# Attention and MLP on one core: the first loads in a row on one queue, the bulk loads held until a first product, less warm work

## The chip, the cores and the metric

The kernel runs on one core of a Trainium2 chip. A core has a matrix engine (TensorE, PE in the profile), a vector engine (VectorE, DVE), an activation engine (ScalarE, ACT), a general engine (GpSimd, POOL) and a queue engine (SyncE, SP). Each works through its own instructions in order. PE writes to PSUM, and DVE and ACT read from there. SP, ACT and POOL issue DMAs, each on a queue of its own, and all queues use the same 16 DMA engines.

The metric is the device time of one execution in microseconds, as the median of several runs. Lower is better.

## The reference: what is computed

```python
# q, k, v: (8, 12, 448, 64) float32;  w_in: (768, 2048);  w_out: (2048, 768)
scores = (1 / sqrt(64)) * (q @ k.transpose(0, 1, 3, 2))
attn = maximum(scores, 0) ** 2 / 448
x = (attn @ v).transpose(0, 2, 1, 3).reshape(3584, 768)
h = x @ w_in
out = (0.5 * h * (1 + erf(h / sqrt(2)))) @ w_out        # (3584, 768) float32
```

There are eight batches of twelve heads. There is no softmax: the scores are clipped at zero and squared. The result of attention, with the heads side by side, goes through an MLP with an exact GELU.

## The kernel before, in words

**Tiling.** The twelve heads of a batch make three groups (g = 0, 1, 2) of four heads. Each group has seven key blocks of 64 rows for each head. q and k must lie with the head dimension on the partitions, so they are transposed: for batches 0 and 1 on PE, as products with an identity matrix `ident` (lines 676, 680, 708 and 715), with a copy from PSUM to SBUF behind each (line 566 on DVE); for the later batches by the DMA engines. A step of attention is one product of k and q into PSUM (line 819), one clipping on ACT (line 831) or on DVE (line 833), and one squaring on DVE (line 841). After seven steps, the products with v follow (line 881). The MLP's first layer stands in line 940, plain blocks of its second in line 1399, and grouped forms of both layers behind.

**The order of the work.** All work after the start is given as operations to `Scheduler`, numbered in the order in which they are added. `ORDER` (lines 91 to 171) is a hand-fixed list of these numbers, each with a letter for its engine: P is PE, A is ACT, D is DVE, G is POOL, S is SP, and Z is a filler product of so many columns on PE. `place()` (line 359) takes the words one after the other, so that each engine's instructions stand in the order of its words. The times in the operations (such as 4.95 in line 1502) are the planner's own estimates and due times; with every operation named in `ORDER`, they change no instruction.

**The bulk loads.** POOL issues the loads that turn float32 into bfloat16 on the way: k (line 605), q (line 514), v (line 623), w_in (lines 529 to 531), w_out (line 535). Its order begins G0 (k of group 1), G1 (q of group 1), G7 (the second half of the sequence of q of group 0), G4 (q of group 2), G108 (q of batch 1, group 0), then `make_ident()`, G2 (v of group 0), G3 (k of group 2). Each load uses one of eight semaphores in turn, so the ninth waits for the first.

**The first loads.** The first half of q of group 0 and the k of group 0 do not go through POOL. They come as float32 through the queues of SP and ACT into `q32` and `k32` (lines 1450 to 1453). k comes in two pieces, key blocks 0 to 3 (`first`, `K_CUT = 4`) and 4 to 6 (`rest`). ACT casts q (A10), DVE the first piece of k (D13) and ACT the rest (A16).

**The first steps.** P11 transposes that half of q (line 708), and D12 copies it to `qT`. P14 and P17 transpose the two pieces of k (line 676), and D15 and D18 copy them to `kT`. P29, P32, P35 and P38 are the products of the first half of q with the seven key blocks, two blocks each and one in P38; A30, A33 and A36 clip the first three and D39 the last. P19 (line 680) and P21 (line 715) transpose k and q of group 1, which G0 and G1 bring; D20 and D22 copy them. P27 does so for the second half of q of group 0. P62 is the first product of group 1, and A63 clips it. On PE the order is P11, P14, P17, P29, P32, P38, P19, P21, P35, P27, P62; on ACT A10, A16, A30, A33, A36, A63; on DVE D13, D12, D15, D18, D39, D20, D22.

**Warm work.** While the first loads are under way, PE runs `SPIN = 11` products of a zero matrix of 512 columns (line 1472), and then the filler Z1056, three products on a quarter of the array with 1056 columns in all (line 1626).

**The identity.** DVE clears `ident` at the start (line 1456), and POOL sets its diagonal by an `affine_select` (line 1459), which stands in its order behind the five loads.

**The weights of the second layer.** G222, G223 and G225 load w_out in three parts; G223 and G225 are two DMAs each. The first readers of all three parts are the plain blocks of output columns 0 to 383 (line 1399, third and fourth block in time). G261 and G262 load k and q of batch 3, group 1.

Of the kernel before, what the change touches and what calls it, by code (L numbers as in the profile page):

```python
# [8 lines left out]
F32 = mybir.dt.float32  # L9
# [3 lines left out]
B, H, S, D = 8, 12, 448, 64  # L13
# [28 lines left out]
NB = 512  # L42
# [45 lines left out]
SPIN = 11  # L88
# [3 lines left out]
D13 G0 Z1056 A10 G1 G7 G4 A16 G108 G1469 P11 D12 P14 D15 P17 P29 P32 D18 P38 D39 P19 P21 A30 D20 P35  # L92
D22 P27 A33 P62 D31 P77 A36 D40 D28 A63 P59 D34 P44 P25 G2 G3 A78 A60 D37 D45 G111 P121 P65 A66 P71
A72 P47 P74 A75 D79 A48 D122 D64 D67 P23 D73 P50 D24 D26 P68 G107 P41 A51 P98 A69 D76 A99 D61 D52
D70 P53 P123 G5 G115 G112 A42 A43 G8 G116 A54 G6 P95 P86 A96 A87 P80 D46 D124 A81 A82 P89 P92 P119
D55 D97 D49 D90 P125 P83 A93 A84 D120 P56 G109 G110 G113 P152 D126 D88 G135 D85 A57 A153 P101 P127
A58 A102 D91 P129 P143 D94 D100 D103 P158 A144 A159 P104 A105 A106 G132 P146 D130 D147 D128 S213
P229 P170 P182 D183 G9 A230 P155 A171 D154 A156 P227 G114 P140 A141 D160 P194 P164 D165 A195 A228
P237 P149 P173 G131 P200 G134 P239 A238 P241 D145 A150 A201 A174 D148 D157 A240 P176 A177 D151 D142
D172 P161 D184 A162 A242 D166 P179 P167 P235 P233 D175 D178 D163 D180 P197 P206 G118 A168 A236 D169  # L100
A198 D181 A234 P185 D207 P203 A186 P188 P231 A187 A232 P243 D214 G221 P247 A244 S212 A248 D202 D204
P249 A250 P245 D189 A246 P257 P272 D199 D205 P191 P269 D192 A258 A273 A270 G117 P255 A256 D190 G138
P251 P266 D196 D193 S215 P275 A276 D208 S216 D267 A252 P209 A210 P281 P284 A211 P356 P340 A282 G133
D217 D285 P290 P305 P308 D291 D292 A357 P342 G137 G260 A341 A309 P344 G259 G136 D283 D306 A343 A345
P253 P299 P293 P278 D268 D286 D279 D280 D271 A254 P350 A351 P352 A353 P358 A359 S219 D220 P346 A347
D300 D301 D277 P362 A363 P366 P364 P302 D294 S218 D274 D295 P317 D303 P287 A318 A367 P329 P296 A365
A288 D310 A330 D304 D307 D289 D297 P360 A361 P354 A355 G222 P370 G223 G225 G261 P326 S389 D390 P314
A315 P332 D333 A327 P372 P323 S388 P320 G262 A321 G264 G224 A371 D380 D298 P311 P439 S392 D324 D328
D322 D381 P430 P368 D383 A373 D384 A312 D334 D313 D316 A369 P348 A349 P338 A431 A339 P377 D382 A378
D385 A440 P411 S395 A412 G139 P445 D387 G226 A446 D325 D441 D407 G399 D386 P436 D331 D408 P433 P374  # L110
A375 A437 A434 P415 G263 G403 D393 D409 S391 P413 P457 P460 A461 S379 D319 D414 P335 P442 D458 P451
A336 A416 A452 P417 P419 D459 A443 A337 S394 D432 D396 D447 D418 D410 P454 P463 D420 P427 A428 P421
P423 P475 G265 D435 D553 D438 A455 A464 D429 P466 D444 G398 P448 D424 A476 D467 D422 G400 D456 G405
P478 P484 P521 G404 G397 G402 A485 D479 D462 D468 D477 A449 P525 D465 D453 A522 S532 A450 P469 P481
D533 A526 P487 A488 A470 P511 A482 S531 P517 P493 D471 P490 S538 P472 D494 D495 D483 S535 A491 A512
G540 D473 G401 A518 D474 P606 P594 P529 A607 A595 P519 A530 P597 P591 P603 A520 P527 D551 D552 D489
A604 D480 D605 A528 G545 P501 A502 P513 A514 D592 D608 D598 S534 P505 A506 G542 P507 P600 D492 D593
P609 D486 P496 A610 D536 A508 A497 D601 G406 A498 P627 P630 D631 P523 A628 D602 A524 S537 S539 P615
P618 P633 P503 P509 D632 A619 G548 D611 A634 A504 D635 P515 D629 A510 D596 P499 P621 D599 A616 S376
A500 A622 P624 G541 D625 P612 A516 A613 S696 D620 P657 D614 D617 D626 P645 A658 S702 G550 P555 A646  # L120
A556 G544 D554 S426 S695 P557 P559 D697 S425 D623 P757 S699 G710 P639 P636 A758 D640 G547 P648 D558
A560 P760 D637 A761 P561 A638 P563 D641 D562 G708 D700 G705 D659 P654 A649 D650 G706 P772 P651 A773
D564 D571 A655 P565 A652 D566 D573 D572 P567 D568 P766 P754 P642 A643 A767 D656 G546 G549 S698 G709
P575 D653 D644 P577 P769 D774 D768 D647 S701 A576 A755 P778 A779 D770 D762 P660 P763 G712 P790 A764
A661 A791 P579 D578 S569 P581 D756 P787 P793 D771 D574 A580 A662 P796 A794 A797 D582 D765 D780 D792
A788 P583 S703 D759 D584 D789 P585 P808 G543 G707 S827 P802 A803 P775 P784 S829 G842 D809 P781 D586
P587 P669 S826 D795 D828 A782 D783 G837 A776 A777 D798 A785 D714 A670 P805 S830 P814 A815 D786 D806
S833 P799 P811 D810 D588 P817 S831 S570 D800 D801 D804 P667 A818 P671 A812 A668 P870 A871 D807 P867
P873 D816 D874 A868 P677 A672 P876 P820 P864 D819 A678 P691 A692 A877 P689 G711 P673 D875 D872 D821
D715 G838 S832 P891 D813 A865 D822 D892 G840 G713 P894 P823 A690 P879 D824 A895 A674 D896 P900 A880  # L130
P665 A825 D834 P663 G843 G839 D866 A901 G835 G836 G704 P882 P888 A666 D869 A664 P903 A889 A883 P683
S937 S940 A684 D893 P687 P693 P927 D717 D878 A904 S942 P897 D881 D884 A928 P885 P906 D898 A688 A694
S943 D907 P921 P679 S941 S590 A680 P685 S939 D899 G841 D905 A922 D938 P681 A686 D944 S936 P718 D902
A682 D908 S589 D716 P675 A719 D890 D929 P722 A676 D923 A886 A887 P915 P912 P1000 A916 D913 P720
A1001 D917 P964 D914 P909 A965 D721 D1002 A723 P958 D966 P924 A910 G945 P724 A959 D925 A911 D960
P952 P976 D725 P930 A953 P726 D977 A931 D926 P918 P946 D932 A919 P728 D727 A947 D734 P979 D920 P933
A980 D729 D735 P955 D948 P949 A934 P730 A956 D950 A935 D957 P961 P994 D951 P1009 A962 P738 D731 A995
D963 S733 D954 P740 A1010 D739 S732 D736 P742 D741 D737 D996 P997 A743 P988 P967 D998 A989 D1011
P985 P1006 A968 D999 P744 A986 D1007 A969 D981 P1012 P973 P970 A1013 D745 P746 D974 A971 D1008 P1003
P982 A1004 D747 P748 D1014 A983 D1005 P750 D749 D984 S752 D972 P848 D975 D987 P1015 A849 D978 D990  # L140
D1018 P991 A1016 A1017 D1026 P852 A992 D1019 A993 D1027 P1030 D1021 P1049 A1031 P1051 D1028 A1050
P1144 D1052 P1068 A1145 D844 P1034 A1069 D751 P1125 A1035 D1022 P1055 A1126 P1148 D845 P1053 D1056
A1149 P1072 D1029 A1054 P1106 A1073 D1025 P1087 A1107 D1023 P1089 A1088 P1110 D1090 P1091 A1111 D846
P1093 A1092 D1020 P850 D1094 D847 P1061 D851 P1099 D1024 A853 P1127 P1032 D1062 P1095 D1128 A1063
P1108 D1033 D1096 P856 D1109 A1098 D1100 P1036 D1242 A1101 P1131 D1037 P854 D1132 D1243 P1137 D855
P1042 D1138 P1163 D857 A1139 P1038 D1043 A1164 P860 D1039 A1044 D1244 A1041 P1102 D861 P1133 D1245
P1129 D1134 P1045 A1130 D1103 P1167 A1136 D1046 A1105 P1165 A1168 P1070 A1048 D1166 P858 P1057 A1040
D859 P1140 A1047 D1071 S862 A1135 P1169 D1058 A1097 P1146 A1104 D1141 S753 A1059 P1064 D1170 A1142
A1143 P1112 D1147 A1060 S863 P1074 D1065 D1113 P1314 A1066 A1067 D1075 P1076 A1315 P1118 D1077 P1080
D1119 A1078 P1150 A1079 D1081 A1120 P1152 D1151 A1082 P1171 D1153 P1156 D1172 A1155 P1175 A1154  # L150
D1157 A1174 P1178 A1173 D1176 A1158 P1318 D1179 A1177 P1114 A1180 D1182 P1159 A1181 D1184 P1186
D1183 D1115 P1263 A1187 D1185 P1083 A1116 D1160 A1264 P1188 A1117 D1084 A1162 A1161 A1085 P1190
A1086 D1189 P1316 A1191 P1192 D1317 P1331 D1193 P1121 A1332 P1194 D1122 A1123 A1124 P1333 D1195
P1265 D1202 P1198 D1204 D1203 P1267 D1334 P1196 D1199 D1205 D1266 P1320 D1197 P1335 D1321 S1200
P1206 S1201 P1208 A1207 P1210 D1209 P1212 A1211 P1337 D1213 P1214 D1224 D1338 P1325 D1215 P1216
D1222 D1326 D1223 P1342 D1217 P1365 D1343 P1218 S1220 A1366 P1226 A1268 D1219 A1327 D1225 S1221
A1344 P1367 D1227 A1336 P1269 A1319 D1368 P1280 D1270 P1228 A1281 P1284 D1229 P1369 A1285 P1322
A1370 P1282 D1323 P1230 D1283 P1328 A1231 P1286 D1329 P1297 D1287 P1299 A1298 P1291 D1300 P1274
D1292 P1232 D1275 A1293 A1276 P1246 D1233 P1303 A1247 P1236 D1304 P1350 D1237 P1371 P1308 P1234
D1309 A1310 P1250 D1372 P1288 D1235 A1251 P1348 S1240 D1289 P1238 P1301 A1324 D1239 P1271 A1330  # L160
S1241 P1294 A1349 D1272 A1302 P1376 D1351 A1290 P1352 D1295 A1273 P1354 D1377 A1353 P1248 A1296
# [1502 lines left out]
```

## Time and profile before

| | us |
|---|---|
| median of 3 runs | 364.42 |
| lowest and highest run | 363.8 and 364.9 |
| the profiled execution, its own time | 364.71 |
| its span in the trace | 362.9 |
| PE busy in the span | 354.5 (98%) |
| DVE busy | 296.4 (82%) |
| ACT busy | 211.3 (58%) |
| POOL busy | 67.2 (19%) |
| DMA, mean over the span | 121 GB/s, 43.83 MB |

The profile is of one execution. Times in the trace count from the span's start. Busy shares are means over stages with different limits, so the start is read from the timeline and not from the shares. Loads of q, k and v through POOL read float32 and write bfloat16; the profile counts what they write. A wait for several semaphores is put down to the one that came last.

### The profile page before, as it was taken

The page shows a single profiled execution, that of the slowest core. Times are in us where ns is not written, and L with a number is a line of the kernel's source. Part 1 is how long each engine was busy: PE and PEld are TensorE (multiplying, and loading weights), DVE is VectorE, ACT ScalarE, POOL GpSimd, SP SyncE. Part 2 cuts the span into 40 slices and gives each one's busy share as a digit, 9 for nine tenths or more (in the row PEclk, how much of TensorE's full clock was granted, in tenths as well). Part 3 has the DMA queues.
Part 4 walks back from the last instruction along what each step waited for, and adds up shares of the span by engine and source line. Part 5 has one row for each costly group of instructions (what it writes and reads, how often), then busy time and mean ns, then how long its engine had stood idle before and what let it go on. Part 6 is the DMA issues. An engine that isn't in the chain of part 4 may idle for free.

```text
span 362.9 us, 7646 instructions
## 1 busy us (share of the span) xinstructions
PE 354.5 (98%) x3103; PEld 190.5 (52%) x3103; DVE 296.4 (82%) x497; ACT 211.3 (58%) x354; POOL 67.2 (19%) x102
## 2 busy tenths in 40 slices
PE   8789999999999999999999999999999999999996
PEld 3464544555554545554454555555555555555663
DVE  2999878869999978999979999998966655786552
ACT  3999766446679685777867864715741233661110
POOL 8566084110911151070000000000000000000000
PEclk9999999999999999999999999999999999999999
DMA  9999999999999999999960421000402120302233
GB/s 165 201 202 199 189 166 193 175 196 199 160 194 163 188 201 171 210 171 202 207 114 4 80 83 45 3 0 3 129 0 63 43 69 2 87 2 87 86 90 88
DMA packets 72260, 43.83 MB, mean 121 GB/s; under 512 B 36385, under 2 KB 69025, under 8 KB 72225
## 3 DMA queue, kind: packets, MB, share of 16 engines
q0 software_dynamic: 32032, 22.47, 43.0%
q1 hardware_dynamic: 39296, 20.03, 28.9%
q10 hardware_dynamic: 896, 0.85, 0.7%
q8 instruction: 24, 0.39, 0.4%
q14 instruction: 12, 0.09, 0.1%
HBM read 45.61 MB, written 11.01 MB: 156 GB/s over the span
## 4 chain that ended last, share of the span: by engine, by line
PE 90%; DVE 3%; ACT 3%; DMA 2%; issue 1%; ACTq 0%; DVEq 0%
PE pso L1281 32%; PE psh L940 21%; PE pb L1092 18%; PE ps L819 9%; PE pav L881 7%; PE pso L1399 3%; ACT a_sq L831 3%; DMA k<-in_k_dram 2%; DVE a_sq L841 1%; DVE osb L1315 1%; DVE a_sq L833 1%; DVE qT L566 0%; ACT xT L568 0%; PE tp L715 0%; DVE s_sb L1260 0%
## 5 line engine op out<-in xcount | busy, mean ns | idle before, releaser
L831 ACT ACTIVATE a_sq<-ps 128x896 bf16<-128x896 f32 x122 | 107.2, 923 | 28.3 <-PE ps L819 26.6
L841 DVE TENSOR_TENSOR a_sq<-a_sq 128x896 bf16<-128x896 bf16 x169 | 96.6, 616 | 2.0 <-ACT a_sq L831 1.6
L940 PE MATMUL psh<-xT,win_sb 128*128 128x448 bf16 x384 | 77.1, 353 | 0.0
L833 DVE TENSOR_SCALAR a_sq<-ps 128x896 bf16<-128x896 f32 (+1 forms) x47 | 50.5, 1077 | 13.4 <-PE ps L819 13.1
L1281 PEld LDWEIGHTS <-s_sb 128*128 128x128 bf16 x424 | 40.4, 98 | 29.7 <-issue 3.5
L940 PEld LDWEIGHTS <-win_sb 128*128 128x128 bf16 x384 | 35.6, 98 | 38.0 <-issue 7.0
L1123 DVE TENSOR_TENSOR part<-pb,part 128x448 f32<-128x448 f32 x80 | 46.5, 619 | 9.0 <-PE pb L1092 6.2
L819 PE MATMUL ps<-qT,kT 64*64 64x448 bf16 (+1 forms) x700 | 48.1, 350 | 2.5 <-ACT a_sq L831 2.0
L950 ACT ACTIVATE h_sb<-psh 128x448 bf16<-128x448 f32 x64 | 34.5, 548 | 19.0 <-PE psh L940 19.0
L1315 DVE TENSOR_TENSOR osb<-pso,p_sb 128x384 f32<-128x384 f32 x39 | 21.6, 554 | 23.6 <-PE pso L1281 18.1
L1281 PEld LDWEIGHTS <-h_sb 128*128 128x128 bf16 x296 | 28.2, 98 | 21.5 <-issue 3.0
L1281 PE MATMUL pso<-t_sb,s_sb 128*128 128x384 bf16 x208 | 38.1, 326 | 0.0
L1144 ACT ACTIVATE h_sb<-part 128x448 bf16<-128x448 f32 (+1 forms) x48 | 24.5, 537 | 22.8 <-DVE part L1123 22.7
L1281 PE MATMUL pso<-wout_sb,s_sb 128*128 128x384 bf16 (+1 forms) x208 | 37.7, 324 | 0.0
L881 PE MATMUL pav<-a_sq,v_sb 64*64 64x448 bf16 (+1 forms) x700 | 36.0, 342 | 0.8 <-ACT a_sq L831 0.8
L1281 PE MATMUL pso<-wout_sb,h_sb 128*128 128x384 bf16 x192 | 35.2, 326 | 0.0
L819 PEld LDWEIGHTS <-kT 64*64 64x64 bf16 x700 | 18.6, 105 | 25.5 <-issue 18.9
L1092 PEld LDWEIGHTS <-win_sb 128*128 128x128 bf16 x192 | 18.8, 98 | 16.7
L881 PEld LDWEIGHTS <-v_sb 64*64 64x64 bf16 x700 | 20.7, 107 | 12.4 <-issue 2.1
L1092 PE MATMUL pb<-xs,ws 128*128 128x448 bf16 x96 | 21.9, 352 | 0.0
L1092 PE MATMUL pb<-xs,win_sb 128*128 128x448 bf16 x96 | 21.8, 352 | 0.0
L1092 PE MATMUL pb<-xT,win_sb 128*128 128x448 bf16 x96 | 21.8, 352 | 0.0
(73 smaller groups left out, 312.4 us busy)
## 6 DMA issues: line engine op xcount, KB each, us to landing
nk<-in_k_dram POOLq DMA_DIRECT2D x23, 224.0 KB, 8.9
nq<-in_q_dram POOLq DMA_DIRECT2D x23, 224.0 KB, 8.5
v_sb<-in_v_dram POOLq DMA_DIRECT2D x4, 672.0 KB, 9.7
out_dram<-osb SPq DMA_DIRECT2D x7, 336.0 KB, 3.3
v_sb<-in_v_dram POOLq DMA_DIRECT2D x10, 224.0 KB, 7.9
out_dram<-osb SPq DMA_DIRECT2D x7, 288.0 KB, 3.4
out_dram<-osb SPq DMA_DIRECT2D x7, 240.0 KB, 2.9
win_sb<-in_moe_w_in_dram POOLq DMA_DIRECT2D x8, 192.0 KB, 9.1
```

The source lines that it names most:

```text
L819: nc.tensor.matmul(ps[64 * j : 64 * j + 64, e, x * w : x * w + w], kT[r, g, i * 128 + 64 * j : i * 128 + 64 * j + 64], moving, start=True, ...
L831: A.activation(ar, ps, AF.Relu, scale=c_att)
L833: V.tensor_scalar(ar, ps, c_att, 0.0, op0=mybir.AluOpType.mult, op1=mybir.AluOpType.max,)
L841: V.tensor_mul(box["a2"][:, :, :used], ar, ar)
L881: nc.tensor.matmul(pav[0][o2 : o2 + 64, e, :w], get_v()[r, 2 * v_slot(b, g) + e, bass.ts(i, D)], box["a2"][r, y, o : o + w], start=(i == 0 ...
L940: nc.tensor.matmul(ph[:, x * n : x * n + n], win_sb[:, kd, bass.ts(m + x, 128)], xT[b][:, kd, c], start=(kd == 0), stop=(kd == KD - 1),)
L950: A.activation(h_ring()[:, m : m + nm, o + c.start : o + c.stop], box[0][:, :S].rearrange("p (x n) -> p x n", x=nm), AF.Gelu,)
L1092: nc.tensor.matmul(ps[name][:, :S], w[:, k, bass.ts(mm, 128)], right()[:, k], start=first and k == 0, stop=k == K1 - 1, skip_group_check=n ...
L1123: V.tensor_add(get(to), ps[name][:, :S], get(other))
L1144: A.activation(to(), src()[:, n0:n1], AF.Gelu)
L1281: nc.tensor.matmul(box[bank][:, n0:n1], left()[:, kf], right()[:, kf, n0:n1], start=bool(need) and kf == 0, stop=kf == K2 - 1, skip_group_ ...
L1315: V.tensor_add(out()[:, n0:n1], box[bank][:, n0:n1], other()[:, n0:n1])
```

## The change

Six edits, all but one at the start:

1. The three first loads go in a row on SP's queue: q, the first piece of k, the rest of k. Before, the two pieces of k went on ACT's queue.
2. `make_ident()` moves in `ORDER` from behind POOL's fifth load to ahead of its first. It is number 1468 now, since the filler is gone.
3. `ident` is cleared only after a first warm product `hold`: DVE copies one column of that product into `ident`, and then clears it. POOL's `affine_select` waits for that clearing, and with it the first bulk load, G0, and everything behind it on POOL.
4. Warm work is less: `hold`, seven products of 512 columns and one of 256, in place of eleven of 512, and the filler Z1056 is left out.
5. G225, the last part of w_out, is issued behind G261 and G262 in place of ahead of them.
6. The planner's times for the three casts are other numbers; no instruction hangs on them.

The rest of `ORDER` has the same words in the same order; its lines are only broken elsewhere.

```diff
-SPIN = 11
+SPIN = 7
...
-D13 G0 Z1056 A10 G1 G7 G4 A16 G108 G1469 P11 D12 P14 D15 P17 P29 P32 D18 P38 D39 P19 P21 A30 D20 P35
+G1468 D13 G0 A10 G1 G7 G4 A16 G108 P11 D12 P14 D15 P17 P29 P32 D18 P38 D39 P19 P21 A30 D20 P35 D22
...
-A288 D310 A330 D304 D307 D289 D297 P360 A361 P354 A355 G222 P370 G223 G225 G261 P326 S389 D390 P314
-A315 P332 D333 A327 P372 P323 S388 P320 G262 A321 G264 G224 A371 D380 D298 P311 P439 S392 D324 D328
+D310 A330 D304 D307 D289 D297 P360 A361 P354 A355 G222 P370 G223 G261 P326 S389 D390 P314 A315 P332
+D333 A327 P372 P323 S388 P320 G262 G225 A321 G264 G224 A371 D380 D298 P311 P439 S392 D324 D328 D322
...
     first = slice(0, K_CUT * D)
-    nc.scalar.dma_start(k32[:, :, first], kv_view(k, 0, 0, 1)[:, :, first])
     nc.sync.dma_start(q32, q_view(0, 0, 1, 0, HC))
+    nc.sync.dma_start(k32[:, :, first], kv_view(k, 0, 0, 1)[:, :, first])
     rest = slice(K_CUT * D, NK * D)
-    nc.scalar.dma_start(k32[:, :, rest], kv_view(k, 0, 0, 1)[:, :, rest])
+    nc.sync.dma_start(k32[:, :, rest], kv_view(k, 0, 0, 1)[:, :, rest])
     zero = const.tile([128, 128], BF16, tag="zero", name="zero")
     V.memset(zero, 0.0)
-    V.memset(ident, 0.0)
...
     spin = banks.take("spin")
-    for _ in range(SPIN):
-        wide = zero[:, :1].to_broadcast([128, NB])
-        nc.tensor.matmul(spin[:, 0], zero, wide, start=True, stop=True)
+    wide = zero[:, :1].to_broadcast([128, NB])
+    hold = f_pp.tile([128, NB], F32, tag="f", name="hold")
+    nc.tensor.matmul(hold, zero, wide, start=True, stop=True)
+    V.tensor_copy(ident[:, :1], hold[:, :1])
+    V.memset(ident, 0.0)
+    for n in (NB,) * SPIN + (NB // 2,):
+        nc.tensor.matmul(spin[:, 0, :n], zero, wide[:, :n], start=True, stop=True)
     banks.give(spin)
```

More of the change, by code (lines that the diff above doesn't have):

```diff
@@ L97 @@
[L97 to L106, printed above, removed]
@@ L112 @@
[L112 to L116, printed above, removed]
@@ new lines @@
+P1150 A1079 D1081 A1120 P1152 D1151 A1082 P1171 D1153 P1156 D1172 A1155 P1175 A1154 D1157 A1174
+P1178 A1173 D1176 A1158 P1318 D1179 A1177 P1114 A1180 D1182 P1159 A1181 D1184 P1186 D1183 D1115
+P1263 A1187 D1185 P1083 A1116 D1160 A1264 P1188 A1117 D1084 A1162 A1161 A1085 P1190 A1086 D1189
+P1316 A1191 P1192 D1317 P1331 D1193 P1121 A1332 P1194 D1122 A1123 A1124 P1333 D1195 P1265 D1202
+P1198 D1204 D1203 P1267 D1334 P1196 D1199 D1205 D1266 P1320 D1197 P1335 D1321 S1200 P1206 S1201
+P1208 A1207 P1210 D1209 P1212 A1211 P1337 D1213 P1214 D1224 D1338 P1325 D1215 P1216 D1222 D1326
@@ L171 @@
+P1436 D1435 D1442 P1438 D1443 D1437 S1440 P1446 D1439 D1445 S1441 P1448 A1447 P1450 D1449 P1452
+A1451 S1463 P1454 D1453 P1456 D1455 S1464 D1458 P1459 D1457 S1465 P1460 D1461 S1466 D1462 S1467
 """
@@ L1501 @@
     src = q32.rearrange("p h (c d) -> p (h c) d", d=D).rearrange("p (e x) d -> p x e d", e=2)
-    o = early("ACT", lambda: by_head(nat_q(0, 0)[:, :, : HC * D]), src, 4 * HC * D, 4.95)
+    o = early("ACT", lambda: by_head(nat_q(0, 0)[:, :, : HC * D]), src, 4 * HC * D, 3.7)
     for c in range(HC):
@@ L1506 @@
     ld_k[0, 0] = []
-    for eng, i0, i1, t in (("DVE", 0, K_CUT, 5.1), ("ACT", K_CUT, NK, 5.45)):
+    for eng, i0, i1, t in (("DVE", 0, K_CUT, 4.4), ("ACT", K_CUT, NK, 5.1)):
         src = k32.rearrange("p e (i d) -> p i e d", d=D)[:, i0:i1]
```

128 lines of the change are left out of this document (67 added, 61 removed).

## The prediction, made before the result was known

> **What bounds the kernel now.** I read first the page's head and the busy time in four stretches (stretch, length, busy us and count on PE, PE loads, DVE, ACT, POOL, then clock, DMA share, GB/s).
>
> ```profile
> span 362.9 us, 7646 instructions
> ```
> ```profile
> 0.00:26.00 26.00, 21.78 (x391) 12.85 (x392) 19.02 (x39) 20.31 (x30) 18.14 (x31) 1.00 1.20 189
> 26.00:60.00 34.00, 33.67 (x339) 16.55 (x331) 28.49 (x44) 26.74 (x43) 18.06 (x26) 1.00 1.30 187
> 60.00:352.00 292.00, 291.78 (x2331) 156.35 (x2330) 245.74 (x409) 163.75 (x282) 30.99 (x47) 1.00 0.64 107
> 6.00:13.00 7.00, 5.82 (x136) 3.93 (x135) 5.48 (x12) 5.30 (x7) 5.29 (x8) 1.00 1.39 193
> ```
>
> From 26 to 352 us PE is idle 0.33 + 0.22 us. So whatever the first 26 us gain or lose reaches the end nearly whole, as long as no load comes late; everything the change touches, but one load, is issued in the first 6 us. The profiled execution took 364.71 us (span 362.9 and 1.8 around it), 0.29 above the median of 364.42. A measurement of this kernel can tell about 0.3%, 1.1 us, from no change.
>
> Next the timeline of the start, engine by engine (start, length): the queues, POOL, PE, ACT, DVE.
>
> ```profile
> 0.74 0.38 SPq L1451 DMA_DIRECT2D q<-in_q_dram  x1
> 0.74 0.49 ACTq L1450 DMA_DIRECT2D k<-in_k_dram  x1
> ```
> ```profile
> 1.24 0.82 POOL L605 DMA_DIRECT2D nk<-in_k_dram  x1 [0.80 <-POOLq L1648]
> 2.06 2.83 POOL L514 DMA_DIRECT2D nq<-in_q_dram  x4
> 4.96 0.32 POOL L1459 TENSOR_SCALAR_AFFINE_SELECT ident<-ident 128x128 bf16<-128x128 bf16 x1
> 5.20 0.73 POOL L623 DMA_DIRECT2D v_sb<-in_v_dram  x1
> ```
> ```profile
> 1.00 4.88 PE L1472 MATMUL spin<-zero 128*128 128x512 bf16 x11 [1.00 <-DVE zero L1455]
> 5.80 0.71 PE L1626 MATMUL fill<-zero 64*64 64x512 bf16 x3
> 6.45 0.37 PE L708 MATMUL tp<-ident,nq 112*128 112x112 bf16 x4
> 6.66 0.39 PE L676 MATMUL tp<-ident,nk 128*128 128x128 bf16 x4
> 7.46 0.34 PE L676 MATMUL tp<-ident,nk 128*128 128x128 bf16 x3 [0.42 <-ACT nk L568]
> 7.74 0.81 PE L819 MATMUL ps<-qT,kT 64*64 64x224 bf16 x20
> 8.48 0.58 PE L680 MATMUL tp<-ident,nk 128*64 128x128 bf16 x14
> 8.89 0.56 PE L715 MATMUL tp<-ident,nq 112*64 112x112 bf16 x16
> 9.38 0.39 PE L819 MATMUL ps<-qT,kT 64*64 64x224 bf16 x8
> ```
> ```profile
> 4.76 0.62 ACT L568 CAST nq<-q 112x512 bf16<-112x512 f32 x1 [1.48 <-DMA q<-in_q_dram]
> 6.90 0.51 ACT L568 CAST nk<-k 128x384 bf16<-128x384 f32 x1 [1.52 <-DMA k<-in_k_dram]
> 8.17 1.73 ACT L831 ACTIVATE a_sq<-ps 128x896 bf16<-128x896 f32 x2 [0.77 <-PE ps L819]
> ```
> ```profile
> 4.99 0.57 DVE L566 CAST nk<-k 128x512 bf16<-128x512 f32 x1 [3.98 <-DMA k<-in_k_dram]
> 6.85 0.39 DVE L566 COPY qT<-tp 128x448 bf16<-128x448 bf16 x1 [1.29 <-PE tp L708]
> 7.16 0.41 DVE L566 COPY kT<-tp 128x512 bf16<-128x512 bf16 x1
> ```
>
> Two things end late. q is cast by 5.38, yet its transposes (P11) start at 6.45: PE is still in warm work. And the rest of k is seen only at 6.90, so P17 starts at 7.46. The chain of waits then runs from these into ACT:
>
> ```profile
> 9.75 0.54 DVE qT L566
> 10.30 0.04 issue
> 10.34 0.41 PE ps L819 x4
> 10.75 0.02 issue
> 10.78 0.93 ACT a_sq L831
> ```
>
> **The change, part by part.** *Less warm work.* Eleven products start at 1.00 and the fill behind them at 5.80, so they follow at 0.436. One held product, seven whole and a half one make 8.5, and PE is free at about 1.00 + 8.5 x 0.436 = 4.7, where now it is free at 6.45. This gives up to 1.75 us, but P11 also needs q's cast.
>
> *q and k in a row on SP.* Issues go at 0.74, 1.12 and 1.50, by SP's 0.38. Packets of each queue in three stretches (4 to 5 us, 5 to 6, 3 to 4; q10 is ACT's, q1 SP's, q0 POOL's):
>
> ```profile
> q10 hardware_dynamic: 257, 0.18, 62.8%
> q0 software_dynamic: 94, 0.08, 57.2%
> ```
> ```profile
> q0 software_dynamic: 233, 0.17, 119.1%
> ```
> ```profile
> q1 hardware_dynamic: 218, 0.10, 35.6%
> ```
>
> q still moved 218 of its 448 packets between 3 and 4 us, beside k. With k behind it in the same row, q should be seen earlier: at best all of those 218 in half the time, at worst as now, so 4.0 to 4.76; I take 4.1. The first part of k then follows at 4.4 to 5.3, as its issue is 0.38 later but the bytes ahead are fewer; I take 4.7, near its 4.99. The rest of k has no bulk packets beside it any more: 5.1 to 6.9; I take 5.4, because 257 of ACT's packets were already through by 5 us and only a few stragglers made it 6.90.
>
> From these, with the durations above: ACT casts q 4.1 to 4.72; P11 starts at 4.75, not 6.45, and at the slow clock of the warm products takes about 0.5. D13 runs 4.7 to 5.27, P14 5.3 to 5.9, the qT copy beside it, the kT copy 5.9 to 6.3. The rest of k is cast by 5.95, P17 runs to 6.35, and the first product of q and k starts at about 6.4 where it is 7.74. The first ACT square starts near 6.85, not 8.17: a head start of 1.3 us.
>
> *The hold.* On POOL the identity now stands ahead of the first bulk load, and waits for DVE, which waits for the first product. That product ends at 1.44 to 1.63; the copy of one column and the memset have no row of their size, so from 0 to two copies of 0.39; I take 0.25, one column being far less than 448. The select holds POOL for 5.20 - 4.96 = 0.24. So the first bulk load is issued at 2.15 instead of 1.24, 0.9 later (0.45 to 1.4). Queued behind it on POOL are the load of q for head group 1 (G1), the other half of q (G7), q of group 2, q of batch 1; from the v load on, 0.24 comes off again: 0.65 later. No other engine's instructions are queued there, but PE waits for two of these loads.
>
> How late do they land? Landings of the first two:
>
> ```profile
> nk<-in_k_dram POOLq DMA_DIRECT2D x1, 224.0 KB, 5.8
> nq<-in_q_dram POOLq DMA_DIRECT2D x1, 224.0 KB, 6.2
> ```
>
> Now k of group 1 lands at 7.04 and q of group 1 at 8.26, 1.2 apart; P19 (8.48) and P21 (8.89) have 1.4 and 0.6 us to spare. If the whole 0.9 passed on, q would land at 9.16, 0.27 after P21's present start. But up to 5 us the bulk queue moved 94 packets, against 233 in the next us: it lost to k what the hold takes away. The first 94 packets are 0.4 us of its own rate, and part of that comes back as k's stragglers no longer lie between. So from +0 to +0.9; I take +0.2, nearer the lower end since that count is a row of this very stretch: k at 7.25, q at 8.46.
>
> **This is where the head start goes.** P19 has its data by 7.3. P21 waits for 8.46 and starts at 8.5, 0.39 before its 8.89; and P35, the eight products at 9.38 that need only early data, stands behind P21 in PE's order and moves with it to 8.99. So ACT, done with its first two squares at 6.85 + 1.73 = 8.58, idles until 9.43, and starts its third 0.4 earlier than now (9.82 to 9.90). The copy of qT follows P21's end, about 0.5 earlier than 9.75. The fourth square on ACT, 10.78 now, starts at about 10.35. From there ACT and DVE are full until 20 us and more, and the lead of about 0.4 stands. It has cover later: the next loads land 0.2 later against work 0.4 earlier, and P21's was the tightest of those I followed.
>
> *One weight piece later.* Two issues of POOL (L535) go behind two others:
>
> ```profile
> 54.11 2.23 POOL L535 DMA_DIRECT2D wout_sb<-in_moe_w_out_dram  x3 [1.36 <-issue]
> ```
> ```profile
> wout_sb<-in_moe_w_out_dram POOLq DMA_DIRECT2D x2, 384.0 KB, 25.2
> ```
> ```profile
> 86.74 2.76 PE L1399 MATMUL pso<-wout_sb,h_sb 128*128 128x384 bf16 x16
> ```
>
> The last piece, issued near 55.5, lands at about 80.7, and its first reader starts at 86.74. Two load issues between cost 1.4 to 3 us: nothing, with 3 us left. Without that cover each us late would be a us lost. The removed fill and the moved wait on ACT's queue cost nothing: ACT idles 1.48 us for q.
>
> Sum: 0.4 by the third and fourth squares, 0.4 to 0.5 by the copy. 364.71 - 0.45 = 364.26 against the profiled execution; 364.42 - 0.45 = 363.97 against the median. I say 364.0.
>
> **The rivals.** *The whole head start passes.* If q of group 1 lands by 7.6, P21 no longer holds P35, and the 1.3 us of the first square remain: 364.42 - 1.3 = 363.1; were it P11's whole 1.7, 362.7. For it: the straggling rest of k delayed this bulk stream. Against it: two loads 1.2 apart behind k leave little way to 7.6.
>
> *The full clock comes late: slower.* The warm products start 0.436 apart, but the fill's 512 + 512 + 32 columns took 0.71 in all and the four transposes 0.37: TensorE got fast near 6 us, after 5 us without a gap (the clock column reads 1.00 throughout, so durations tell this). Now the unbroken stretch ends at 4.7, with transposes and gaps behind it. If PE stays slow, the work between 6 and 13 us, 5.82 busy, grows; a good third of a modelled duration is the pipeline's end (P14 starts 0.21 after P11, whose row says 0.37), so by about two thirds of that, 3.9 us, if slow throughout. Room is the head start of 1.7 and the 1.18 idle there, 2.9. It decides once the fast clock comes later than 6 + 7 x 2.9 / 3.9 = 11.2 us; at 13 the cost is 1.0: 365.4, and 366 if later still. For it: 3.7 us of products where 5 were given. Against it: transposes follow at once, so gaps are 0.1 to 0.5 us.
>
> The Trainium skill speaks for this rival: "TensorE: Matmul & The Clock Gate", Part 1, says that the clock rises after a busy window of about 3.4 us that runs freely, not from the kernel's start, and Part 4 that transposes do not count as busy in the same way. By that rule 3.7 us of products would fill a window only by luck; the trace agrees that 5 us sufficed, and no run here shows what 3.7 do.
>
> *The hold costs what the start gains.* With the bulk loads late by the whole 0.9, P21 starts 0.3 later than now: 364.7. For it: 0.9 is the plain shift in issue. Against it: the 94 packets.
>
> **How the numbers follow.** Forecast (0 to 0.9 gained) 0.50; whole head start 0.26; late clock 0.12; hold 0.12. The first covers 363.5 to 364.4. The range goes from the whole of P11's lead, 362.7, to 365.2, most of the late clock's cost; beyond it lie the late clock's worst cases and little below. Faster by over 1.1 us: nearly all of the whole head start and a little of the forecast, 0.28. Slower by over 1.1: half of the late clock and some of the hold's upper bounds, 0.10. Same 0.62.
>
> **What would show it.** In the new profile: warm products ending near 4.7; P11 at 4.7 to 5.4; the casts of q, k and the rest of k at 4.1, 4.7, 5.4; the first bulk issue near 2.15; P21 waiting for its load at about 8.5, ACT idle before its third square; QK pairs at today's length from 6.4 on (if double, the clock). PE as full as now from 26 us on. It is wrong if P21 starts before 8, if PE is slow beyond 9, or if a new wait of PE for a load appears after 26 us.

## The result, and the profile after

| | before | after |
|---|---|---|
| median of 21 runs each, us | 364.05 | 365.95 |
| lowest and highest | 363.12 and 365.01 | 363.93 and 368.15 |
| the profiled execution, its own time | 364.71 | 364.00 |
| its span in the trace | 362.9 | 362.2 |
| mean granted clock of TensorE | 0.998 or more (85 runs beside the experiments) | 12 runs 0.998 or more, 9 runs 0.979 to 0.995 |

The change makes the kernel slower by 1.9 us: the ratio is 1.0053, with an interval of 1.0040 to 1.0065. The forecast was 364.0, in a range to 365.2. A ratio leaves out runs more than 1.5% above the fastest of the same kernel; here this concerns one run, 370.07 of the hold alone.

The two profiled executions say the opposite, 362.9 before and 362.2 after. They aren't typical: the one of before lies near the top of its runs, the one of after is the second shortest of its 21. First, then, what the profiled execution of after shows, and then what it doesn't.

The page's head and the busy time in three stretches (columns as in the prediction):

```profile
span 362.2 us, 7637 instructions
```
```profile
0.00:26.00 26.00, 20.79 (x386) 12.67 (x387) 19.89 (x41) 20.81 (x31) 18.46 (x31) 1.00 1.18 184
26.00:60.00 34.00, 34.00 (x334) 16.83 (x334) 28.59 (x44) 26.38 (x42) 18.42 (x27) 1.00 1.29 192
60.00:352.00 292.00, 292.00 (x2334) 156.61 (x2332) 244.76 (x409) 163.60 (x281) 30.29 (x46) 1.00 0.63 108
```

From 26 us on PE is full, as before. The difference lies in the start. The timeline of the start, in order of time:

```profile
1.18 0.48 SPq L1450 DMA_DIRECT2D k<-in_k_dram  x1
...
1.70 0.47 SPq L1452 DMA_DIRECT2D k<-in_k_dram  x1
...
2.31 0.82 POOL L604 DMA_DIRECT2D nk<-in_k_dram  x1
...
3.13 2.83 POOL L513 DMA_DIRECT2D nq<-in_q_dram  x4
...
3.64 0.62 ACT L567 CAST nq<-q 112x512 bf16<-112x512 f32 x1 [1.40 <-DMA q<-in_q_dram]
...
4.27 0.56 DVE L565 CAST nk<-k 128x512 bf16<-128x512 f32 x1 [2.28 <-DMA k<-in_k_dram]
...
4.59 0.58 PE L707 MATMUL tp<-ident,nq 112*128 112x112 bf16 x4
...
6.29 0.51 ACT L567 CAST nk<-k 128x384 bf16<-128x384 f32 x1 [2.04 <-DMA k<-in_k_dram]
...
6.86 0.34 PE L675 MATMUL tp<-ident,nk 128*128 128x128 bf16 x3 [1.25 <-ACT nk L567]
...
7.57 1.73 ACT L830 ACTIVATE a_sq<-ps 128x896 bf16<-128x896 f32 x2 [0.76 <-PE ps L818]
...
8.49 0.58 PE L714 MATMUL tp<-ident,nq 112*64 112x112 bf16 x16
...
9.44 1.73 ACT L830 ACTIVATE a_sq<-ps 128x896 bf16<-128x896 f32 x2 [0.15 <-PE ps L818]
```

P11 starts at 4.59, where it stood at 6.45. q and the first k are early. But the rest of k is seen only at 6.29, and P17, which needs it, leaves PE idle for 1.25 us. Of the 1.86 us that P11 gained, 0.60 are left at P17 (6.86 for 7.46), 0.40 at P21 (8.49 for 8.89). The chain of waits goes through the same load:

```profile
1.70 4.57 DMA k<-in_k_dram
6.27 0.02 issue
6.29 0.52 ACT nk L567
6.81 0.05 issue
6.86 0.34 PE tp L675 x3
```

How the row's last load strands can be seen in the packets of after, from 0 to 4 us, 4 to 5, and 5 to 6 (q1 is SP's queue, which has all three first loads now; q0 is POOL's):

```profile
q1 hardware_dynamic: 922, 0.63, 51.6%
...
q0 software_dynamic: 56, 0.05, 69.6%
q1 hardware_dynamic: 75, 0.05, 15.1%
...
q0 software_dynamic: 185, 0.14, 106.4%
q1 hardware_dynamic: 11, 0.01, 2.9%
```

The row has 922 of its 1008 packets through by 4 us. The last 86, which by their order should be the rest of k, take 2.3 us more, while the bulk load's packets run on the same DMA engines. Further down, a kernel that holds the bulk load longer bears out that this load is what holds them up.

### The profile page after: what moved, and what is told of

Same layout as the page of the kernel before. It is cut to its first block, busy times and chain, and to the rows that moved or that the text cites. A ratio compares the mean times of both kernels' runs of the same rounds, so it can differ in the third digit from the quotient of the medians.

```text
span 362.2 us, 7637 instructions
## 1 busy us (share of the span) xinstructions
PE 353.2 (98%) x3098; PEld 190.3 (53%) x3098; DVE 296.3 (82%) x498; ACT 211.3 (58%) x354; POOL 67.2 (19%) x102
## 4 chain that ended last, share of the span: by engine, by line
PE 93%; ACT 4%; DMA 1%; issue 1%; DVE 0%; SPq 0%
PE pso L1280 33%; PE psh L939 21%; PE pb L1091 18%; PE ps L818 10%; PE pav L880 8%; ACT a_sq L830 3%; PE pso L1398 3%; DMA k<-in_k_dram 1%; PE tp L714 0%; ACT xT L567 0%; DVE osb L1314 0%; DVE a_sq L840 0%; PE tp L679 0%; ACT nk L567 0%; SPq L1450 0%
```

## The experiments

Each kernel ran beside runs of the kernel before on the same chip; medians of before were 363.6 to 364.1. A ratio is against those. "a4" below is a landmark of the prediction: the start of ACT's fourth operation on the scores, which clips them and which the prediction calls a square (10.78 in the trace of before, 10.26 in that of after).

**Each part alone.** First the row without the hold and with the old warm work:

```diff
-    nc.scalar.dma_start(k32[:, :, first], kv_view(k, 0, 0, 1)[:, :, first])
     nc.sync.dma_start(q32, q_view(0, 0, 1, 0, HC))
+    nc.sync.dma_start(k32[:, :, first], kv_view(k, 0, 0, 1)[:, :, first])
...
-    nc.scalar.dma_start(k32[:, :, rest], kv_view(k, 0, 0, 1)[:, :, rest])
+    nc.sync.dma_start(k32[:, :, rest], kv_view(k, 0, 0, 1)[:, :, rest])
```

> The kernel before with the three first loads in a row on SP alone; warm work, identity and bulk loads as before. Theory C: no loss, 363.6 to 364.4, since the warm work covers all. Theory H, as far as it is the row: 365 or more.

Measured: 367.66 (365.68 to 369.78, 6 runs), ratio 1.0099 (1.0064 to 1.0134). This is the dearest single part: 3.65 us. Five of the six runs have less than the full clock (0.984 to 0.997); the one with the trace has 0.998. The timeline of its trace, and its waits of PE in the first 20 us (in total, times, longest):

```profile
3.34 0.62 ACT L568 CAST nq<-q 112x512 bf16<-112x512 f32 x1 [1.11 <-DMA q<-in_q_dram]
...
7.64 0.51 ACT L568 CAST nk<-k 128x384 bf16<-128x384 f32 x1 [3.69 <-DMA k<-in_k_dram]
```
```profile
PE tp L676 <- ACT nk L568: 2.1, 1, 2.1
```

q is seen 1.4 us earlier than in the trace of before, the rest of k 0.7 later, and 2.3 us later than in the next kernel, whose k is on ACT's queue. P17 waits for it.

Less warm work alone, eight products of 512 columns and one of 256, and no filler:

```diff
-SPIN = 11
+SPIN = 8
...
-    for _ in range(SPIN):
+    for n in (NB,) * SPIN + (NB // 2,):
...
-D13 G0 Z1056 A10
+D13 G0 A10
```

> The kernel before with less warm work alone: eight and a half products and no filler; loads, queues and identity as before. Theory C: slower by 1 to 2 us, 365.0 to 366.0, with runs spread over 3.5 us or more, though no load is held. Theory H: no loss, 363.6 to 364.2, spread as before.

Measured: 364.43 (363.35 to 365.1, 12 runs), ratio 1.0004 (0.9990 to 1.0018). Its trace has a span of 361.6 and one of the earliest starts of all:

```profile
5.38 0.51 ACT L568 CAST nk<-k 128x384 bf16<-128x384 f32 x1
...
7.13 4.25 ACT L831 ACTIVATE a_sq<-ps 128x896 bf16<-128x896 f32 x5 [1.24 <-PE ps L819]
...
7.78 0.56 PE L715 MATMUL tp<-ident,nq 112*64 112x112 bf16 x16
```

P21 starts at 7.78 without a wait: the whole head start passes, and ACT runs five squares in a row (a4 9.66). And yet the median doesn't fall. So 8.5 products, short as they are, can bring the full clock in time: the four transposes of P14 take 0.39 us in this trace, as in that of before. No run loses the clock afterwards (all 12 have 0.998 or more).

The hold alone (before, with the first product held, `make_ident()` ahead of G0, eleven products and the filler kept):

```diff
-D13 G0 Z1056 A10 G1 G7 G4 A16 G108 G1469 P11
+G1469 D13 G0 Z1056 A10 G1 G7 G4 A16 G108 P11
```

> The kernel before with the held identity and bulk loads alone; k on ACT's queue, warm work as before. Theory R (the rest of k, third in one row and sharing the slowest DMA engine with the bulk queue, lands late and at changing times; that is the loss, and the hold only softens it): no loss from the hold, 363.6 to 364.6, spread about 2 us. Theory H (the hold itself costs, through the bulk loads that come later): 364.8 to 365.6.

Measured: 364.74 (364.04 to 370.07, 6 runs), ratio 1.0024 (1.0008 to 1.0039): 0.9 us by the ratio, 1.1 between the medians. Its waits of PE hold a new one, for q of group 1:

```profile
PE tp L715 <- DMA nq<-in_q_dram: 0.3, 1, 0.3
```

The issue list of this trace gives that load 5.3 us from issue to landing, so from 3.13 it lands at 8.43; with less warm work alone it is issued at 2.06, takes 5.4 and lands at 7.46. Of the 1.07 us of later issue 0.97 reach the landing, and P21 starts at 8.47 for 7.78. A second trace of the same kernel:

> The kernel before with the hold alone, for a second trace. Theory G: above 364.5 us PE waits for q of group 1 at P21 by more than the 0.3 us of the first trace, or for a load after 26 us; the clock stays, since the warm work runs to 5.6 us.

It took 364.19: P21 at 8.50, with 0.41 of wait for q of group 1, a4 at 10.26. The same. But these two starts are no worse than that of the kernel before with only the rest of k on SP's queue (below: P21 at 8.40, a4 at 10.28; the first product of the MLP at 27.67, here at 27.74 and 27.65), and the first trace is of the shortest of its six runs. So these traces show the wait, but not where the longer runs lose their time.

The weight piece, put back to its old place in the kernel after:

```diff
-G223 G261 P326
+G223 G225 G261 P326
...
-P320 G262 G225 A321
+P320 G262 A321
```

> The changed kernel with the weight piece G225 back in its old place. If the later piece costs nothing and gives nothing, as predicted: 365.4 to 366.5, the changed kernel's time, with as wide a spread. If it costs: under 365.2. If it gives: over 366.7.

Measured: 366.09 (365.23 to 367.38, 6 runs), ratio 1.0059 (1.0037 to 1.0081), as after itself. And the other way round, moved later in the kernel with less warm work:

> The kernel before with less warm work and the later weight piece, without row and hold. Theory G: no loss, 363.5 to 364.4, within 0.3% of the kernel before; a gain of 0.3 to 0.6 us at best, as the first product of q and k moves up by 1.0 us in the trace of less warm work alone but P21 still has to wait for its load.

Measured: 364.46 (363.37 to 367.94, 12 runs), ratio 1.0020 (1.0000 to 1.0040); trace as without it (P21 7.80, span 361.6). In each pair the intervals overlap, so no effect of the move is to be seen.

**After, with one part undone.** The warm work of before put back, ten products of 512 columns behind the held one and the filler, with the row and the hold kept:

```diff
-SPIN = 7
+SPIN = 10
...
-    for n in (NB,) * SPIN + (NB // 2,):
+    for n in (NB,) * SPIN:
...
-G1468 D13 G0 A10
+G1469 D13 G0 Z1056 A10
```

> The changed kernel with the warm work of before: the held product, ten more of 512 columns and the filler of 1056. Theory C (TensorE's full clock comes late or is lost in most executions, since the shorter warm work does not fill one of its free windows): the loss goes, 364.0 to 364.6, and the runs lie as close as those of before, within about 2 us. Theory H (the held bulk loads or the row on SP cost the time): it stays slow, 365.5 to 366.5, spread of about 4 us.

Measured: 365.0 (364.4 to 366.05, 8 runs), ratio 1.0033 (1.0022 to 1.0045). All eight runs have the full clock; of after's 21, nine have not.

k back on ACT's queue, with the hold and the short warm work kept:

> The changed kernel with k back on ACT's queue and nothing else undone: hold, less warm work and the later weight piece stay. Theory R: the loss goes, 363.4 to 364.4, spread about 2 us. Theory H: it stays, 365 or more. Theory C (the clock): 364.4 to 365.5 with a wide spread.

Measured: 364.81 (364.22 to 367.68, 6 runs), ratio 1.0040 (1.0015 to 1.0065), full clock in all. In its trace the rest of k is seen at 4.92 and the first square starts at 6.67, 1.5 before that of before. Then P19 waits 0.24 us for k of group 1 and P21 0.51 for q of group 1 and starts at 8.30. Later PE waits for one more load of q:

```profile
12.35 0.58 PE L714 MATMUL tp<-ident,nq 112*64 112x112 bf16 x16 [0.42 <-DMA nq<-in_q_dram]
```

Without the hold this kernel is the one above, less warm work with G225 later, whose trace has none of these waits. There P21 starts at 7.80 and the first product of the MLP at 26.96; here at 8.30 and 28.07. So in this pair of traces the hold alone takes 1.1 us of the start.

Two mixed forms of the row. Only the rest of k on SP's queue, in the kernel before:

> The kernel before with only the rest of k moved to SP, behind q; the first piece of k stays on ACT. Theory R: most of the row's loss comes already, 365 to 367 with a spread over 2.5 us, if standing behind q is enough; 364.0 to 364.6 if it takes all three in one row.

Measured: 364.36 (363.88 to 365.02, 6 runs), ratio 1.0017 (1.0002 to 1.0032). The rest of k is seen at 5.54, so it isn't SP's queue as such that is slow. Third place in it isn't enough either, as the long hold shows below. With less warm work, q and the first k on SP, the rest on ACT:

> The kernel before with less warm work, q and the first piece of k in a row on SP, the rest of k alone on ACT, nothing held. Theory G: q is seen near 3.7 as in the changed kernel, the rest of k no later than before, bulk loads as before: 363.2 to 364.2, the best case for both kernels. If a row on SP is slow whatever stands in it: 365.5 or more.

Measured: 364.68 (363.61 to 365.52, 12 runs), ratio 1.0018 (1.0006 to 1.0029). All three loads are early (q 4.36, rest of k 4.88) and no load is waited for at P21, but P11 waits 0.53 us for the identity, which is still made behind five loads, and the transposes of P21 take 0.96 us in its trace, where they take 0.56 in that of less warm work alone: the clock came late. One of the 12 runs is below the full clock (0.995).

**The clock.** Two more traced executions of the kernel after itself. Between them a third took 1276.35 us, with PE busy for 1270.5 us where the trace of after has 353.2; why isn't known, and of its start only one landing is used below.

> The changed kernel once more, for a second trace. Theory G: in a trace above 365.5 us the rest of k or q of group 1 lands at least 0.7 us later than in the first trace (6.27 and 8.47), and where the granted clock is under 0.997 a stretch at half clock follows one with PE idle for a load.

> The changed kernel a third time, for the same question as the look before: which landing is late in a slow execution, and whether half clock follows the idle stretch.

> The changed kernel once more for a trace. Theory G: if it is above 365.5 us, a stretch with PE waiting for k or for bulk loads between 5 and 10 us, and half clock behind it or a wait for a load after 26 us; if it is below 364.5, neither.

The first took 367.44 and the last 365.17. The first one's timeline of PE:

```profile
6.43 0.34 PE L675 MATMUL tp<-ident,nk 128*128 128x128 bf16 x3 [1.00 <-ACT nk L567]
...
8.04 0.58 PE L679 MATMUL tp<-ident,nk 128*64 128x128 bf16 x14 [0.53 <-DMA nk<-in_k_dram]
9.19 0.96 PE L714 MATMUL tp<-ident,nq 112*64 112x112 bf16 x16 [0.57 <-DMA nq<-in_q_dram]
10.08 0.59 PE L818 MATMUL ps<-qT,kT 64*64 64x224 bf16 x8
```

and its stretches:

```profile
5.00:8.50 3.50, 1.97 (x43) 1.29 (x41) 1.71 (x4) 1.87 (x3) 3.29 (x6) 1.00 1.28 162
8.50:12.00 3.50, 2.93 (x50) 1.79 (x44) 2.44 (x6) 1.53 (x3) 2.62 (x4) 0.50 1.35 187
12.00:16.00 4.00, 3.72 (x64) 2.53 (x57) 3.66 (x6) 2.77 (x4) 2.20 (x5) 0.50 1.26 204
```

PE has three waits in 3 us: for the rest of k (the row), for k of group 1 and for q of group 1 (the hold). From 5.0 to 8.5 it is busy for only 1.97 of 3.50 us, and then the granted clock falls to a half, until 18.77 us. P21's transposes take 0.96 for 0.58, a4 is at 11.75 and the span 365.6. The last of the three has the same three waits (1.27, 0.24, 0.57), keeps its clock, and has a4 at 10.79 and a span of 363.4. So the busy time of such a stretch doesn't decide by itself. The same stretch in this trace, and in that of the row alone, which keeps its clock too:

```profile
5.00:8.50 3.50, 1.94 (x41) 1.14 (x39) 1.58 (x5) 1.75 (x3) 3.45 (x6) 1.00 1.30 165
```
```profile
5.00:8.50 3.50, 1.36 (x18) 0.77 (x18) 0.72 (x2) 0.51 (x1) 3.06 (x5) 1.00 1.38 197
```

PE is no busier in either than in the trace that lost its clock. Where in time the idle microseconds must lie to cost the clock, these traces don't show.

The trace of the kernel with G225 put back shows a third form. There no clock is taken away; it comes late:

```profile
7.07 0.50 PE L675 MATMUL tp<-ident,nk 128*128 128x128 bf16 x3 [1.48 <-ACT nk L567]
7.50 1.15 PE L818 MATMUL ps<-qT,kT 64*64 64x224 bf16 x20
8.58 0.96 PE L679 MATMUL tp<-ident,nk 128*64 128x128 bf16 x14
9.33 0.96 PE L714 MATMUL tp<-ident,nq 112*64 112x112 bf16 x16
```

PE waited 1.48 us for the rest of k, and everything up to 10.2 us runs at slow lengths (1.15 for the 0.81 of the twenty products), with a4 at 11.51. The clock column reads 1.00 in this stretch, as it did in the prediction's rows: it shows what is taken away, not what hasn't yet come.

If waits cost the clock, longer ones should cost it more often. The hold behind four products in place of one:

```diff
+    for _ in range(4):
+        nc.tensor.matmul(spin[:, 0], zero, wide, start=True, stop=True)
     hold = f_pp.tile([128, NB], F32, tag="f", name="hold")
...
-SPIN = 7
+SPIN = 3
```

> The changed kernel with the held product behind four others, so that bulk loads are issued about 1.7 us later still, near 4.0, and the first loads have the DMA engines to themselves. The identity is still ready for P11. Theory R: the rest of k lands at 5.3 or sooner and the spread falls under 2 us; the later bulk loads cost about 1 us by P21, so 364.8 to 365.6. If the row is slow by itself, without the bulk queue: the rest of k still lands at 6 or later, spread 4 us, 366.5 or more.

Measured: 367.41 (366.01 to 368.1, 6 runs), ratio 1.0098 (1.0080 to 1.0116). All six runs have less than the full clock, 0.984 to 0.995, where the kernel after, with as many products and a hold behind the first, is below 0.998 in 9 of 21. In its trace P19 and P21 wait 1.07 and 1.06 us for the held loads, and the clock falls at 9.43 and comes back at 16.26:

```profile
6.00:9.40 3.40, 1.49 (x37) 0.87 (x34) 1.80 (x4) 1.73 (x2) 3.40 (x6) 1.00 1.29 158
9.40:12.80 3.40, 3.14 (x44) 1.92 (x45) 2.14 (x5) 1.49 (x2) 3.22 (x5) 0.50 1.33 176
12.80:16.30 3.50, 3.22 (x60) 2.25 (x56) 3.16 (x6) 2.27 (x4) 2.03 (x3) 0.51 1.26 202
```

The same trace shows what holds up the rest of k. The bulk load is issued at 4.02 here, and the rest of k, third in the row as before, is seen at 5.20, so P17 doesn't wait:

```profile
5.20 0.51 ACT L567 CAST nk<-k 128x384 bf16<-128x384 f32 x1 [0.84 <-DMA k<-in_k_dram]
```

By 4 us 885 of the row's packets are through, fewer than in the trace of after, but the other 123 follow by 5 us. So the same third place gives 7.64 with the bulk load issued at 1.24, 5.59 to 6.51 with it at 2.31 (seven traces; 5.06 in the execution of 1276 us), and 5.20 with it at 4.02; the first and the last are one trace each. And here the clock is lost with the waits for the two held loads alone, without one for the rest of k.

And the opposite: PE kept busy in those waits, by a filler of 1536 columns ahead of P17, then by two (1536 ahead of P17, 1024 ahead of P19):

```diff
-P14 D15 P17 P29 P32 D18 P38 D39 P19
+P14 D15 Z1536 P17 P29 P32 D18 P38 D39 Z1024 P19
```

> The changed kernel with one filler of 1536 columns between the transposes of the two pieces of k, where PE idled 1.25 us; P11 starts as early as in the changed kernel. Theory C: the filler closes the gap, so 363.4 to 364.2 and a spread of about 2 us, at or below the kernel before. Theory H: 365.5 to 366.5, since loads and queues are as in the changed kernel.

> The changed kernel with a filler of 1536 columns ahead of P17 and one of 1024 ahead of P19, so that PE works through both places where it waits for loads. Theory G (late loads leave PE idle in the stretch in which the clock is decided, and the lost clock is the larger part of the loss): every run keeps the clock (0.998 and more), 364.0 to 364.9. If the late loads themselves are the larger part: the clock is kept and the time stays at 365.2 to 366.

Measured: 365.5 (364.48 to 366.42, 7 runs), ratio 1.0040 (1.0025 to 1.0055), and 365.41 (364.64 to 369.9, 11 runs), ratio 1.0061 (1.0033 to 1.0088). With one filler three of seven runs still have less than the full clock (0.993 to 0.995), and PE waits 0.7 and 0.5 us for the held loads in its trace. With two, three of eleven have (0.995), and in the one of them that has a trace the clock isn't lost in the start but after a wait at 115 us, told of next. Eight of eleven full clocks against twelve of 21 don't show that the fillers help, and the kernel stays slower than before with them.

**Where the head start of less warm work goes.** The filler left out alone, eleven products kept:

> The kernel before without the filler Z1056, all eleven products kept; queues, identity and loads as before. If the warm work is long enough at 4.7 us to bring the clock in time: P11 near 5.7, up to 0.5 us better, 363.4 to 363.9, and a spread as before. If not: 364.0 to 364.6 with a wider spread, as with eight and a half products.

Measured: 364.2 (363.28 to 365.94, 11 runs), ratio 1.0013 (0.9997 to 1.0028). And a second trace of less warm work:

> The kernel before with eight and a half products and no filler, for a second trace. Theory G: above 364.3 us the full clock comes later than 7 us or P21 waits for its load; below 363.8 neither, as in its first trace.

It took 363.53, with span 361.7. The start of the two is the same (P21 at 7.77 and 7.85). But the profiled execution without the filler took 365.02, with a span of 363.2. Its timeline shows where 1.2 of the 1.5 us went:

```profile
102.96 1.23 SPq L742 DMA_TRANSPOSE kT<-nk  x1
...
115.07 0.38 PE L819 MATMUL ps<-qT,kT 64*64 64x448 bf16 x4 [1.23 <-DMA kT<-nk]
```

and the waits of SP's queue between 93 and 110 us:

```profile
SPq L742 <- DMA nk<-in_k_dram: 9.6, 1, 9.6
```

PE waits at 115 us for the transposes of a later k, which the DMA engines make and SP issues once a bulk load has landed. The list of issues gives them, from issue to landing,

```profile
kT<-nk SPq DMA_TRANSPOSE x1, 12.1
```

that is 102.96 + 12.1 = 115.06. The timeline of the first trace of less warm work alone, where PE doesn't wait:

```profile
101.47 1.22 SPq L742 DMA_TRANSPOSE kT<-nk  x1
...
113.69 0.55 PE L819 MATMUL ps<-qT,kT 64*64 64x448 bf16 x8
```

There the transposes take 10.4 us and land at 111.87, 1.8 ahead of PE. Over the nineteen traces of this case, without that of 1276 us, they land between 106.8 and 117.3 us, and PE comes at 113.6 to about 117. It waits in four: 1.23 here, 0.46 with the rest of k on SP's queue, 1.84 with two fillers (where half a clock follows, from 118.3 to 121.7), 0.2 in the first further trace of after. In two more, less warm work with G225 later and the second trace of the hold, the data come 0.02 and 0.05 us ahead of PE. In the trace of before PE comes at 114.81, with less warm work alone at 113.6 to 113.8: of a landing at 115.06 the first would wait 0.25 us, the second 1.3 to 1.5. So a head start runs, in some executions, into a stream of loads that doesn't start earlier with it.

## Why the prediction was wrong

**The start, step by step.** Warm work's end and P11 came as said (4.75 forecast, 4.59 measured). q came at 3.64 (4.1 forecast, 4.0 to 4.76 the bounds) and the first k at 4.27 (4.7): better than said. The first bulk load was issued at 2.31 (2.15), k and q of group 1 landed at 7.31 and 8.43 (7.25 and 8.46), P21 started at 8.49 (8.5), ACT's third square at 9.44 (9.43), a4 at 10.26 (10.35). For this one execution the number comes out, 364.26 forecast and 364.00 measured, but in part by luck. The execution is the second shortest of 21. And the first square came at 7.57, not 6.85: most of the head start was gone before P21, at the rest of k, so ACT idled only 0.15 us ahead of its third square where 0.85 was forecast. Of the signs of being wrong that the prediction names, "PE is slow beyond 9" is met in the first further trace of after and in that with G225 put back.

**The step that failed first: "The rest of k has no bulk packets beside it any more ... I take 5.4."** It came at 6.29, inside the bounds of 5.1 to 6.9 but 0.9 later than the sum took it, and P17 waited 1.25 us. In the seven traces with the row and this hold it comes at 5.59 to 6.51 (5.06 in the execution of 1276 us). Third in the row, it is issued at 1.70, and the bulk load, issued at 2.31, does run beside its last packets: without the hold it comes at 7.64, with the long hold at 5.20. On ACT's queue it comes at 4.88 to 5.56 in the eight traces beside that of before. The prediction's 257 packets are those from 4 to 5 us; by 5 us 533 of the 544 of ACT's queue were through, so eleven stragglers made it 6.90 in the trace of before. None of the eight shows that, so the row was credited with removing what is usually not there (before itself has one trace, so how rare it is isn't known).

**The step that failed second: the hold, "I take +0.2".** Its own landings came as said, but the 0.2 was counted from landings at 7.04 and 8.26 which were again those of that execution. In the traces with the old issue beside that of before and that of the row alone (8.46), q of group 1 lands at 7.3 to 7.8. Against that the later issue passes to the landing nearly whole (0.97 of 1.07), and where the start is early enough to meet it, as with k back on ACT's queue, the hold takes 1.1 us. Alone in the kernel before it costs 0.9 by the ratio, though its two traces show only the wait. The rival "the hold costs what the start gains" named this mechanism, with a price of 364.7 by landings that aren't usual.

**The sign.** P21 at 8.49 and a4 at 10.26 looked like a gain over 8.89 and 10.78. The trace of before with only the rest of k on SP's queue, where that load comes at 5.54, has P21 at 8.40 and a4 at 10.28. That is what I take the usual start of before to be (an argument from that neighbour; before itself has one trace): the best start of after only equals it, and the others are worse, a4 at 10.79, 11.51 and 11.75.

**The rival with the right sign, and its reason.** "The full clock comes late: slower" gave 365.4, and 366 if later still; 365.95 was measured. But its reason, 3.7 us of products being too few, isn't enough by itself. With 8.5 products and the old queues and issues, the three traces have the full clock by P14 (0.39 to 0.42 us), and none of 24 runs (with and without the later G225) loses it; and the row alone is below the full clock in five of six runs with all the warm work in place. What goes with a lost clock are the waits behind the warm work, for the rest of k or for the two held loads; the long hold, which lengthens two of them, loses it in all six runs. Yet the short warm work has its part. With row and hold, eight of eight runs with the old warm work have the full clock, and 12 of 21 with the short one. And in two traces with the short one, G225 put back and the split row, the full clock came only near 10 us, which is this rival's own mechanism. In the 21 runs of after, the nine below 0.998 have a mean of 366.65, the other twelve 365.56.

The prediction cited the Trainium skill, "TensorE: Matmul & The Clock Gate", Part 1, for a window of about 3.4 us. The traces agree: the half clock lasted 3.4 us with two fillers, 6.83 in the kernel with the long hold and 10.24 in the first further trace of after, one, two and three times 3.41. No run here isolates its rule in Part 4, that a transposing TensorE doesn't count as busy in the same way: less warm work alone has transposes right behind its products, and had its full clock in time and kept it.

**"It has cover later."** It has none to spare at 115 us. Here the prediction had followed P21's load and one weight piece, not the k whose transposes SP issues, nor the q that PE waits for at 12.35 once k is back on ACT's queue. This can explain why the less warm part, right in its start, gains nothing that the median shows: one trace, of its neighbour without the filler, shows 1.23 us given back. How many runs do so isn't shown.

**What adds up, and what stays open.** Over before, by the medians: the row alone 3.65, the hold alone 1.1, less warm work 0.4 within an interval that includes zero, G225 nothing that can be seen. They don't add: the hold takes the row's worst back, and row and hold with the old warm work cost 1.0. The step from there to after, 0.9, goes with the clock, which is whole in eight of eight runs there and in 12 of 21 here. Undoing the row alone leaves a ratio of 1.0040 (1.0015 to 1.0065) of the 1.0053, so what the row costs within the whole change isn't clear of the noise. No kernel tried has row and less warm work without the hold. Not settled is what the twelve full-clock runs of after lose, 1.5 us over before. Against the usual start (the neighbour's first product of the MLP at 27.67) the three traces with a full clock, of after twice and with G225 put back once, have it at 27.64, 28.17 and 28.89: nothing, 0.5 and 1.2 later. What is above that could be a full clock that comes still later, which the mean granted clock doesn't show, or waits at 115 us; no trace divides them. None of the kernels tried is faster than before.

## What to carry to other kernels

The last load of a row is late when a bulk load starts beside its tail, so the load that the matrix engine needs next must not stand last there; and a hold on the bulk loads is paid by their readers, unless these have slack in a usual execution, not only in the one that was profiled. Before costing an edit against a start in which loads compete, set the one profiled execution against its runs, and treat an unusual landing in it as an accident that the edit will not remove. Waits of a microsecond in the first ten can cost more than themselves: in some executions half clock followed them, for 6.83 and 10.24 us.

## What the runs showed of the hardware that was not expected

- The granted clock fell to a half after a stretch of about 3.4 us in which PE was busy for 1.49 (of 3.40) or 1.97 (of 3.50) us, and stayed there for 6.83 and 10.24 us, though PE was then busy for 3.14 of 3.40 us and 3.72 of 4.00. In two other traces PE was busy for 1.94 and 1.36 of 3.50 us in the same part of the start, and the clock stayed.
- Moving one load to another issuing engine moved landings by more than its issue: the rest of k, issued at 1.70 in the row and at 1.27 in the trace of before, came at 7.64 as third on SP's queue, at 5.54 on it as second, at 4.88 to 5.56 as second on ACT's or alone there. The Trainium skill, "DMA: Bandwidth & Descriptors", section "Issuing engines are not separate DMA queues", says that issuing on several engines saves only the issuing time; here the row alone cost 3.65 us (ratio 1.0099, 1.0064 to 1.0134), and the measurement decides.
- With the bulk load issued at 2.31, the DMA engines moved 922 of the row's 1008 packets by 4 us and needed until 6.27 for the other 86. With it issued at 4.02, they moved 885 by 4 us and the other 123 by 5 us.
